# Row maximum of attention scores: a copy, three maxima and a 32x32 transpose replaced by one VectorE reduction with built-in transpose

## Chip, core and metric

The kernel runs on one core of one Trainium2 chip. The metric is the device time of one execution in microseconds, measured on that core. Engines are named as in the profile: PE is TensorE's matmul side and PEld its weight loads, DVE is VectorE, ACT is ScalarE, POOL is GpSimd, and SP is the queue that issues nearly all DMA transfers.

## The reference

Causal attention for 8 batches of 12 heads, 448 positions and a head width of 64, followed by a soft mixture of experts over all 3584 tokens:

```python
scores = scale * np.matmul(q, k.transpose(0, 1, 3, 2))
scores = np.where(mask, -1000000000.0, scores)          # causal
scores = scores - np.max(scores, axis=-1, keepdims=True)
attn = np.exp(scores)
attn = attn / (np.sum(attn, axis=-1, keepdims=True) + 1e-09)
attn_out = np.matmul(attn, v)
...
x = attn_out.transpose(0, 2, 1, 3).reshape(B * S, H * D)   # 3584 x 768
logits = x @ phi                                           # 32 slots, 4 per expert
d = exp(logits - logits.max(0)); d /= d.sum(0)             # dispatch
c = exp(logits - logits.max(1)); c /= c.sum(1)             # combine
slot_input = d.T @ x
for e in range(8):
    h = np.maximum(slot_input[e] @ w1[e], 0.0)
    slot_out[e] = h @ w2[e]
out = c @ slot_out
```

The change touches `np.max(scores, axis=-1)` only: for each query the maximum over its keys.

## The kernel before

**Two parts.** The first part runs over the 96 heads, two to a pair; the second runs the experts with their 64 weight tiles and writes the output. The logits and the dispatch of a batch are worked into the first part, by a table `plan` that says behind which head each piece stands.

**One head.** Scores are kept with keys on the partitions and queries in the columns. A head's tile `s` is one PSUM tile of 128 x 1024: the four chunks of 128 keys lie side by side, each only as wide as causality lets it be (448, 320, 192 and 64 queries), at the columns `SCOL`, so that 1024 columns are all used. There are three such tiles. `scores1` writes the mask (`c0`, `c12`, `c3`) and the products of the rounded `qd` and `ks` (`k0` to `k3`). Then the maximum of each query, over all keys, is taken in these steps:

- `max_evac` (`ev`): ACT copies chunk 0, 448 columns, out of PSUM to the SBUF tile `mx`.
- `max_keys` 0 to 2 (`x0` to `x2`): DVE takes the maximum of `mx` with chunks 1, 2 and 3 (320, 192 and 64 columns), in place. Each partition then holds the maximum of up to four keys.
- `max_keys` 3 (`x3`): DVE transposes `mx` in blocks of 32x32 to the tile `mt`; `max_keys` 4 (`x4`) reduces each block of 32 columns to one number. The result `r`, 128 x 14, holds for 14 blocks of 32 queries the maximum over each group of 32 partitions.
- `max_row` 0 (`mr0`): PE transposes `r` to `rt`; `max_row` 1 (`mr1`): DVE takes the maximum over the four groups, negated, to `mr`, 14 x 32.
- `max_spread` (`sp`): POOL spreads `mr` into 14 rows of the operand `r2`.

`scores2` (`t0` to `t3`) then adds to the same PSUM tile, by one more matmul per chunk with `k2` and `r2`, the negated maximum and the remainders of the rounding; `exps` on ACT takes the exponential to `pt`; `attv` (`a0` to `a3`) multiplies by v into the PSUM tile `po`; `norm` (`n0` to `n2`) on DVE divides by the sums. Beside this ACT rounds q and k of a later pair (`cq`, `ck`), POOL subtracts to get the remainders (`sq`, `sk`), and ACT copies `k2` (`c2`).

**The order.** Every engine runs its instructions as they stand in the program (the helper on L69 records each of them, which is why every row of the profile says L69). The table `ORDER` gives the order of the steps, one line for even heads and one for odd ones. The loop is pipelined: at head i it writes the scores of head i + 2 and takes their maxima, does `mr0`, `mr1` and `sp` of head i + 1, `scores2` and the exponential of head i, and `attv` and the normalisation of head i - 1. The heads 0 to 3 are written out by hand ahead of the loop and in its first two rounds.

**Loads.** SP issues its transfers in program order; one that has to wait for a buffer holds all behind it. The loads of q, k and v run up to three pairs ahead, through three buffers of the pool `raw` (3584 bytes per partition each). The weights come as tiles of 128 x 1536 (768 KB): tiles w0 to w22 have memory of their own and are loaded beside the attention. The next twelve, from w23 on, are put into the memory of the attention's own pools (`raw`, `fix`, `wk`, `xtp`, `moe`), which lie at one end of the SBUF one behind the other; each of these loads waits for the last users of whatever lies under its tile. `fix` holds the tiles that live through the whole attention, `mx` and `mt` among them (L106, L107).

Of the kernel before, what the change touches and what calls it, by code (L numbers as in the profile page):

```python
# [9 lines left out]
F32 = mybir.dt.float32  # L10
F32R = mybir.dt.float32r
BF16 = mybir.dt.bfloat16
AF = mybir.ActivationFunctionType
ALU = mybir.AluOpType
AX = mybir.AxisListType
PSUM = bass.MemoryType.PSUM

P = 128
NB, NH, S, HD = 8, 12, 448, 64
# [6 lines left out]
NQB = S // 32  # L26
# [4 lines left out]
NHD = 2 * NPAIR  # L31
# [13 lines left out]


ORDER = (
# [4 lines left out]
)  # L52

SC0, SC1, SC2, SC3 = 512, 0, 320, 960
CQ0 = (0, 128, 256, 384)
SCOL = (SC0, SC1, SC2, SC3)
# [28 lines left out]
def attention_soft_moe(ctx: ExitStack, tc: tile.TileContext, qk, va, phi, w1, w2, out):  # L85
    nc = _Core(tc)
# [6 lines left out]
    xtp = early.enter_context(tc.tile_pool(name="xtp", bufs=1, side="right"))  # L93
    wk = early.enter_context(tc.tile_pool(name="wk", bufs=1, side="right"))
    fix = early.enter_context(tc.tile_pool(name="fix", bufs=1, side="right"))
# [7 lines left out]
    qd_, ks_ = ([fix.tile([P, 2, S], F32R, name=f"{o}0")] for o in ("qd", "ks"))  # L103
    x_[1] = fix.tile([P, NCH, 3 * P], F32, name="x1")
    qd_.append(fix.tile([P, 2, S], F32R, name="qd1"))
    mx_ = fix.tile([P, S], F32, name="mx")  # L106
    mt_ = fix.tile([P, S], F32, name="mt")  # L107
    ks_.append(fix.tile([P, 2, S], F32R, name="ks1"))
    r2_ = [fix.tile([P, 2, S], F32R, name="r20")]
    va_[0] = fix.tile([P, NCH, 2, VC], F32, name="va0")  # L110
# [13 lines left out]
    st = {}  # L124
# [11 lines left out]
    def loads_v(p, eng=nc.sync):  # L136
        if p < NPAIR:
            eng.dma_start(out=va_[p % 2], in_=va[p])
# [49 lines left out]
    ident = const.tile([P, P], F32, name="ident")  # L188
# [8 lines left out]
    po0 = ps_1.tile([P, NCH, VC], F32, name="po")  # L197
    identb = const.tile([P, P], BF16, name="identb")

    zero = mt_[:, 0:P // 2]  # L200
    nc.vector.memset(zero, 0.0)
    nc.vector.tensor_copy(out=identb, in_=ident)
    for i in range(NR):
# [7 lines left out]
    def misc(name):  # L211
        return ps_1.tile([P, 512], F32, tag="m", name=name)
# [10 lines left out]
    def cast_q(p, hs=slice(0, 2)):  # L223
        if p < NPAIR:
            nc.scalar.activation(out=qd_[p % NR][:, hs], in_=st["raw", 0, p][:, hs], func=AF.Copy)

    def cast_k(p, hs=slice(0, 2)):
        if p < NPAIR:
            nc.scalar.activation(out=ks_[p % NR][:, hs], in_=st["raw", 1, p][:, hs], func=AF.Copy)
# [6 lines left out]
    def copy_k2(p, hs=slice(0, 2)):  # L236
        if p < NPAIR:
            nc.scalar.activation(out=k2_[64:P, hs], in_=ks_[p % NR][0:64, hs],
                                 func=AF.Copy)
# [35 lines left out]
        for part in ("c0", "k3", "c3", "c12", "k2", "k1", "k0"):  # L275
            scores1(i, part)

    def max_evac(i):
        if i < NHD:
            st["mx", i] = (xtp.tile([P, 512], F32, tag="xt", name="mx1", bufs=2)[:, 0:S] if i == 1  # L280
                           else mx_)
            nc.scalar.activation(out=st["mx", i], in_=st["s", i][:, SC0:SC0 + S], func=AF.Copy)

    def max_keys(i, k):
        if i >= NHD:
            return
        if k < 3:
            s, mx = st["s", i], st["mx", i]
            c, w = k + 1, S - CQ0[k + 1]
            nc.vector.tensor_tensor(out=mx[:, CQ0[c]:S], in0=s[:, SCOL[c]:SCOL[c] + w],  # L290
                                    in1=mx[:, CQ0[c]:S], op=ALU.max)
        elif k == 3:
            nc.vector.transpose(out=mt_, in_=st.pop(("mx", i)))
        else:
            r = st["r", i] = wk.tile([P, NQB], F32, tag="r", name=f"r{i}", bufs=2)
            nc.vector.tensor_reduce(out=r, in_=mt_.rearrange("p (b k)->p b k", k=32),
                                    axis=AX.X, op=ALU.max)

    def max_row(i, k):
        if i >= NHD:  # L300
            return
        if k == 0:
            st["rt", i] = misc(f"rt{i}")
            nc.tensor.transpose(out=st["rt", i][0:NQB, 0:P], in_=st.pop(("r", i)), identity=ident)
        else:
            mr = st["mr", i] = wk.tile([NQB, 32], F32, tag="mr", name=f"mr{i}", bufs=2)
            nc.vector.tensor_reduce(out=mr, in_=st.pop(("rt", i))[0:NQB, 0:P].rearrange("p (g t)->p t g", g=4),
                                    axis=AX.X, op=ALU.max, negate=True)

    def max_spread(i):  # L310
        if i >= NHD:
            return
        p, h = divmod(i, 2)
        mr = st.pop(("mr", i))

        nc.gpsimd.affine_select(out=r2_[p % NR][0:NQB, h].rearrange("p (b t)->p b t", t=32),
                                in_=mr.unsqueeze(1).to_broadcast([NQB, NQB, 32]),
                                compare_op=ALU.is_equal, fill=0.0, base=0,
                                pattern=[[-1, NQB], [0, 32]], channel_multiplier=1)
# [12 lines left out]
    def exps(i):  # L332
        if i < NHD:
            nc.scalar.activation(out=pt_[i % 2][:, 0:1024], in_=st.pop(("s", i)), func=AF.Exp, scale=SCALE)
# [108 lines left out]
    plan = {}  # L443
# [22 lines left out]
    scores1_all(0)  # L466
    warm(START[1])

    max_evac(0)
    cast_q(0, h1)  # L470
    sub_q(0, h1)
    scores1_all(1)
    warm(START[2])
    copy_k2(0, h0)
    max_evac(1)
    cast_k(1, h0)
    cast_k(1, h1)
    cast_q(1, h0)
    copy_k2(0, h1)
    cast_q(1, h1)  # L480

    for i, k in ((0, 0), (0, 1), (0, 2), (0, 3), (0, 4), (1, 0)):
        max_keys(i, k)
    sub_k(1, h0)
    max_row(0, 0)
    warm(START[5], po0.rearrange("p a b->p (a b)")[:, 0:2 * P])
    scores1_all(2)
    warm(START[3])
    max_evac(2)
    max_row(0, 1)  # L490
    max_spread(0)
    for k in (1, 2, 3, 4):
        max_keys(1, k)
    sub_q(1, h0)

# [27 lines left out]
    for i in range(NHD):  # L523
        p, h = divmod(i, 2)
        if h:
            load_qk(p + 3, 1)
            if p + 1 < NPAIR - 1:
                loads_v(p + 1)
            load_qk(p + 3, 0)
            if p % 2 and nload < RES:  # L530
                load_w(nload)
                nload += 1
        if i == NHD - 3:

            loads_v(NPAIR - 1, nc.scalar)
        if i < 2:
            scores2(i, (1, 0, 2))
            if i:
                scores1_all(3)
                max_evac(3)  # L540
            scores2(i, (3,))
            exps(i)
            if i == 0:
                max_row(1, 0)
                warm(START[4], po0.rearrange("p a b->p (a b)")[:, 0:P])
                max_row(1, 1)
                sub_k(1, h1, nc.vector)
                max_spread(1)
                sub_q(1, h1)

        qs = [int(n[1]) for n in ORDER[h] if n[0] == "a"]
        first = qs[:2] if qs[0] == 3 else qs[:1]
        for n in ORDER[h]:
            if i < 2 and (n in ("ev", "exp") or n[0] in "kt" or n in ("c0", "c3", "c12")):
                continue
            if i == 0 and n in ("mr0", "mr1", "sp"):
                continue
            if n[0] == "k" or n in ("c0", "c3", "c12"):
                scores1(i + 2, n)
            elif n[0] == "t":  # L560
                scores2(i, (int(n[1]),))
            elif n[0] == "a":
                attv(i - 1, (int(n[1]),), first)
            elif n[0] == "x":
                max_keys(i + 2, int(n[1]))
            elif n[0] == "n":
                norm(i - 1, int(n[1]))
            elif n in ("mr0", "mr1"):
                max_row(i + 1, int(n[2]))
            elif n == "ld":  # L570
                if i % 12 == 3 and i > 12:
                    logits_d(i // 12 - 1, lt)
            elif n == "plan":
                if later and i:
                    later.pop(0)()
                plan.get(i, int)()
            else:
                {"ev": lambda: max_evac(i + 2), "exp": lambda: exps(i), "sp": lambda: max_spread(i + 1),
                 "ck": lambda: cast_k(p + 2), "sk": lambda: sub_k(p + 2), "cq": lambda: cast_q(p + 2),
                 "c2": lambda: copy_k2(p + 1), "sq": lambda: sub_q(p + 2)}[n]()  # L580
        if i == NHD - 1:

            scs.close()
            pe = att.enter_context(tc.tile_pool(name="pe", bufs=1, space=PSUM, reuse_waits="tile"))
            ps = [pe.tile([P, 512], F32, name=f"e{k}") for k in range(6)]

    i, b, p = NHD - 1, NB - 1, NPAIR - 1
# [9 lines left out]
    for k, qcs in ((2, (3, 2)), (4, (1, 0))):  # L597
# [6 lines left out]
                                in1=sm[:, cs].unsqueeze(2).to_broadcast([P, 2, HD]), op=ALU.mult)  # L604
# [17 lines left out]
    for c in range(NCH):  # L622
# [11 lines left out]
                            axis=AX.X, op=ALU.min)  # L634
# [21 lines left out]
    for hf in range(2):  # L656
# [7 lines left out]
        else:  # L664
# [8 lines left out]
                            axis=AX.X, op=ALU.add)  # L673
# [139 lines left out]
    n = NBUF  # L813
# [83 lines left out]
```

## Time and profile before

| | |
|---|---|
| timed runs (3) | median 454.3 us, 453.79 to 455.17 |
| span of the profiled execution | 452.4 us; it states no other time |
| instructions | 12067 |
| PE, DVE and ACT busy, 0 to 15 us | 11.52, 9.49 and 10.48 us |
| the same, 15 to 42 us | 26.01, 23.88 and 23.58 us |
| the same, 344 to 380 us | 35.23, 21.83 and 10.69 us |
| the same, 380 to 452 us | 51.32, 28.59 and 21.22 us |
| DMA | 119.04 MB, 263 GB/s over the span |

The attention with its heads ends at about 344 us, the rest is the experts and the output. A row of a group gives the names of output and input with shapes, the number of instructions, then their busy time and the mean time of one, then the engine's idle time ahead of them and what ended most of it. A row of the timeline gives start and length, with idle time and releaser in brackets. In the rows of DMA issues the last number is the time from issue to landing. All times are microseconds, apart from the means, which are in nanoseconds.

### The profile page before, as it was taken

What the parts mean: (1) busy time and instruction counts of PE and PEld (TensorE: products, weight loads), DVE (VectorE), ACT (ScalarE), POOL (GpSimd) and SP (SyncE); (2) the same over time, 40 slices, a digit from 0 to 9 for tenths busy, and PEclk for the clock granted to TensorE, in tenths of its full rate; (3) what the DMA queues carried; (4) which work ended last, traced back from release to release, by engine and by line L of the source; (5) the groups of instructions that cost most, each with busy time, mean ns of one, the idle gap of its engine ahead of it and who ended that gap; (6) DMA issues with size and microseconds to landing.
All of it is one profiled execution on the core that took longest, in us unless ns stands there. A gap on an engine that the chain in (4) does not pass through costs nothing.

```text
span 452.4 us, 12067 instructions
## 1 busy us (share of the span) xinstructions
PE 426.1 (94%) x4628; PEld 365.6 (81%) x4628; DVE 348.6 (77%) x1050; ACT 329.8 (73%) x496; POOL 267.0 (59%) x216
## 2 busy tenths in 40 slices
PE   7999999999999999999999999999999999999750
PEld 3898999999999989998999899989998864544330
DVE  5888888888888888889888888888888457623450
ACT  6898899789988979897889789978995311333340
POOL 5988778777777777777777777877783000000000
PEclk9999999999999999999999999999999999999985
DMA  8377766776767766776577766776667999999998
GB/s 275 132 257 240 226 194 225 240 229 185 224 213 251 236 204 192 236 239 223 172 237 252 225 201 202 222 242 234 198 202 262 419 412 424 421 427 410 403 394 347
DMA packets 34473, 119.04 MB, mean 263 GB/s; under 512 B 3824, under 2 KB 8944, under 8 KB 32880
## 3 DMA queue, kind: packets, MB, share of 16 engines
q1 hardware_dynamic: 34272, 118.01, 74.7%
q8 instruction: 37, 0.61, 0.5%
q10 hardware_dynamic: 144, 0.27, 0.2%
q14 instruction: 20, 0.16, 0.1%
HBM read 107.25 MB, written 11.01 MB: 261 GB/s over the span
## 4 chain that ended last, share of the span: by engine, by line
PE 74%; DMA 12%; POOL 4%; DVE 3%; ACT 2%; issue 1%; SPq 0%; POOLq 0%; ACTq 0%
PE po L69 34%; PE s L69 24%; DMA w<-in_w_dram 10%; PE xt L69 4%; PE g L69 3%; PE sp L69 2%; POOL r L69 2%; PE rt L69 2%; DMA qk<-in_qk_dram 2%; PE e L69 1%; PE pp L69 1%; POOL ks L69 1%; DVE lm L69 1%; PE hp L69 1%; ACT ot L69 1%
## 5 line engine op out<-in xcount | busy, mean ns | idle before, releaser
L69 PE MATMUL po<-va,pt 128*128 128x65 f32 x1900 | 193.5, 250 | 0.1
L69 PEld LDWEIGHTS po<-va,pt 128*128 128x128 f32 x1900 | 190.5, 171 | 0.5 <-issue 0.3
L69 DVE TENSOR_TENSOR mx<-s,mx 128x320 f32<-128x320 f32 (+2 forms) x288 | 100.8, 350 | 30.2 <-ACT mx L69 26.4
L69 POOL TENSOR_TENSOR r<-qk,qd 64x896 fp32r<-64x896 f32 (+1 forms) x50 | 101.5, 2030 | 6.9 <-ACT qd L69 3.0
L69 POOL TENSOR_SCALAR_AFFINE_SELECT r<-mr 14x448 fp32r<-14x448 f32 x96 | 61.9, 645 | 72.1 <-DVE mr L69 71.6
L69 ACT ACTIVATE pt<-s 128x1024 f32<-128x1024 f32 x96 | 98.3, 1024 | 5.5 <-PE s L69 2.6
L69 POOL TENSOR_TENSOR ks<-qk,ks 64x896 fp32r<-64x896 f32 (+1 forms) x47 | 98.1, 2087 | 4.4 <-ACT ks L69 0.8
L69 PE MATMUL s<-r,k 128*128 128x320 f32 (+3 forms) x384 | 83.0, 298 | 1.4 <-POOL r L69 1.3
L69 ACT ACTIVATE mx<-s 128x448 f32<-128x448 f32 x96 | 52.5, 547 | 36.3 <-PE s L69 23.6
L69 PE MATMUL s<-qd,ks 128*128 128x448 f32 (+3 forms) x384 | 75.9, 308 | 1.5 <-ACT qd L69 1.4
L69 DVE STREAM_TRANSPOSE mt<-mx 128x448 f32<-128x448 f32 x96 | 62.0, 645 | 3.3
L69 PEld LDWEIGHTS s<-r,k 128*128 128x128 f32 (+1 forms) x384 | 60.0, 176 | 5.3 <-POOL r L69 2.0
L69 DVE TENSOR_REDUCE r<-mt 128x14 f32<-128x448 f32 x96 | 58.4, 609 | 0.1
L69 PEld LDWEIGHTS s<-qd,ks 128*128 128x128 f32 (+1 forms) x384 | 54.9, 180 | 3.0 <-ACT qd L69 2.2
L69 ACT ACTIVATE ks<-qk 128x896 fp32r<-128x896 f32 (+1 forms) x50 | 45.6, 914 | 2.8 <-DMA qk<-in_qk_dram 2.8
L69 ACT ACTIVATE k<-ks 64x896 fp32r<-64x896 f32 (+1 forms) x49 | 45.8, 935 | 1.1
L69 ACT ACTIVATE qd<-qk 128x896 fp32r<-128x896 f32 (+1 forms) x50 | 46.1, 922 | 0.5 <-DMA qk<-in_qk_dram 0.4
L69 PEld LDWEIGHTS <-identb 128*128 128x128 bf16 x339 | 29.1, 99 | 17.6 <-issue 15.1
L69 DVE TENSOR_TENSOR x<-po,sm 128x256 f32<-128x256 f32 x95 | 40.3, 424 | 3.3
L69 PE MATMUL s<-tri,identb 128*128 128x64 bf16 (+2 forms) x288 | 39.5, 234 | 0.2
L69 ACT ACTIVATE xts<-xt 128x512 f32<-128x512 f32 x47 | 28.2, 600 | 2.8 <-PE xt L69 0.5
L69 PE MATMUL xt<-ident,x 128*128 128x128 f32 x188 | 28.4, 274 | 0.0
(137 smaller groups left out, 398.7 us busy)
## 6 DMA issues: line engine op xcount, KB each, us to landing
qk<-in_qk_dram SPq DMA_DIRECT2D x94, 448.0 KB, 3.5
w<-in_w_dram SPq DMA_DIRECT2D x43, 768.0 KB, 6.1
w<-in_w_dram SPq DMA_DIRECT2D x10, 1536.0 KB, 19.3
va<-in_va_dram SPq DMA_DIRECT2D x47, 260.0 KB, 3.5
out_dram<-ot SPq DMA_DIRECT2D x16, 384.0 KB, 6.7
out_dram<-ot SPq DMA_DIRECT2D x2, 1536.0 KB, 9.2
qk<-in_qk_dram SPq DMA_DIRECT2D x4, 224.0 KB, 3.5
hw<-in_w_dram SPq DMA_DIRECT2D x1, 768.0 KB, 6.6
```

What stands on the lines that cost most here:

```text
L69: return self._tc.keep_in_program_order(op(*args, **kwargs))
```

## The change

ACT's copy is gone. DVE reduces straight from PSUM: `max_keys` 0 is one `tensor_reduce` over all 1024 columns, taken as 32 blocks of 32 and transposed 32x32 on the way (`apply_transpose=True`). Its result `r` is 128 x 32, one column for each block of 32 queries of each chunk. `max_keys` 1 to 3 then take the maximum of chunk 0's 14 columns (16 to 29) with those of the other chunks, over 10, 6 and 2 columns, in place. PE's transpose reads these 14 columns. `mx` and `mt` go; the tile of zeros that lay in `mt` gets one of its own.

```diff
-    ("c3", "c0", "k3", "c12", "k1", "k0", "k2", "t0", "t2", "ev", "x1", "t1", "a0", "a3", "t3", "ck",
-     "mr0", "exp", "x0", "a2", "mr1", "x2", "x3", "a1", "cq", "sp", "n0", "sk", "n1", "ld", "n2", "x4", "plan"),
+    ("c3", "c0", "k3", "c12", "k1", "k0", "k2", "t0", "t2", "t1", "a0", "a3", "t3", "ck",
+     "mr0", "exp", "x0", "a2", "x1", "x2", "x3", "mr1", "a1", "cq", "sp", "n0", "sk", "n1", "ld", "n2", "plan"),
...
-    mx_ = fix.tile([P, S], F32, name="mx")
-    mt_ = fix.tile([P, S], F32, name="mt")
+    zero = fix.tile([P, P // 2], F32, name="zero")
...
-    def max_evac(i):
-        if i < NHD:
-            st["mx", i] = (xtp.tile([P, 512], F32, tag="xt", name="mx1", bufs=2)[:, 0:S] if i == 1
-                           else mx_)
-            nc.scalar.activation(out=st["mx", i], in_=st["s", i][:, SC0:SC0 + S], func=AF.Copy)
...
-        if k < 3:
-            s, mx = st["s", i], st["mx", i]
-            c, w = k + 1, S - CQ0[k + 1]
-            nc.vector.tensor_tensor(out=mx[:, CQ0[c]:S], in0=s[:, SCOL[c]:SCOL[c] + w],
-                                    in1=mx[:, CQ0[c]:S], op=ALU.max)
-        elif k == 3:
-            nc.vector.transpose(out=mt_, in_=st.pop(("mx", i)))
+        if k == 0:
+            r = st["r", i] = wk.tile([P, 32], F32, tag="r", name=f"r{i}", bufs=2)
+            nc.vector.tensor_reduce(out=r, in_=st["s", i].rearrange("p (b k)->p b k", k=32),
+                                    axis=AX.X, op=ALU.max, apply_transpose=True)
         else:
-            r = st["r", i] = wk.tile([P, NQB], F32, tag="r", name=f"r{i}", bufs=2)
-            nc.vector.tensor_reduce(out=r, in_=mt_.rearrange("p (b k)->p b k", k=32),
-                                    axis=AX.X, op=ALU.max)
+            r, c0, c, q = st["r", i], SC0 // 32, SCOL[k] // 32, CQ0[k] // 32
+            rq = r[:, c0 + q:c0 + NQB]
+            nc.vector.tensor_tensor(out=rq, in0=rq, in1=r[:, c:c + NQB - q], op=ALU.max)
...
-            nc.tensor.transpose(out=st["rt", i][0:NQB, 0:P], in_=st.pop(("r", i)), identity=ident)
+            nc.tensor.transpose(out=st["rt", i][0:NQB, 0:P], in_=st.pop(("r", i))[:, SC0 // 32:SC0 // 32 + NQB], identity=ident)
...
-    max_evac(0)
...
-    for i, k in ((0, 0), (0, 1), (0, 2), (0, 3), (0, 4), (1, 0)):
+    for i, k in ((0, 0), (0, 1), (0, 2), (0, 3), (1, 0)):
         max_keys(i, k)
```

The odd line of `ORDER` changes in the same way, and the calls of `max_evac` for heads 1 to 3 in the start go as well. PE's order of instructions stays as it was; ACT and DVE have 96 fewer each.

On DVE, in the round of head 40, these rows stood between two normalisations before the change (`s42` is the tile of head 42, `mr41` belongs to head 41, `po`, `sm` and `x0` to the normalisation; what an instruction waits for is in brackets):

```order
L69 TENSOR_TENSOR x0_101<-po_129,sm38_2294 128x4x64 [waits DVE_49]
L69 TENSOR_REDUCE r41_2304<-mt_90 128x14
L69 TENSOR_TENSOR mx_89<-s42_2313,mx_89 128x192 [waits Activation_49]
L69 TENSOR_TENSOR mx_89<-s42_2313,mx_89 128x320 [waits DVE_49]
L69 TENSOR_REDUCE mr41_2340<-rt41_2333 14x32 [waits PE_49,Pool_49]
L69 TENSOR_TENSOR mx_89<-s42_2313,mx_89 128x64 [waits DVE_49]
L69 STREAM_TRANSPOSE mt_90<-mx_89 128x448 [waits DVE_49]
```

The same place after the change:

```order
L69 TENSOR_TENSOR x0_100<-po_128,sm38_2210 128x4x64 [waits DVE_49]
L69 TENSOR_REDUCE r42_2248<-s42_2227 128x32 [waits PE_49]
L69 TENSOR_TENSOR r42_2248<-r42_2248 128x10 [waits DVE_49]
L69 TENSOR_TENSOR r42_2248<-r42_2248 128x6 [waits DVE_49]
L69 TENSOR_TENSOR r42_2248<-r42_2248 128x2 [waits DVE_49]
L69 TENSOR_REDUCE mr41_2256<-rt41_2245 14x32 [waits PE_49,Pool_49]
L69 TENSOR_SCALAR sm39_2262<-po_128 128x4 [waits PE_49]
```

The reduction waits for PE instead of ACT, and all of the maximum of head 42 now stands ahead of `mr41`; before, the smallest maximum, the transpose and the reduction stood behind it.

On SP, at the end of the attention, the loads of the first weight tiles that overlie the attention's pools stood so before the change (`w22` is the last with memory of its own):

```order
L69 DMA w22_4981<-in_w2_dram 128x1536
L69 DMA w23_5332<-in_w2_dram 128x1536 [waits DMAHW5_49,DMAHW7_49,DMAHW3_49,Pool_49]
L69 DMA w24_5334<-in_w1_dram 128x1536 [waits DMAHW4_49,PE_49]
L69 DMA w25_5336<-in_w1_dram 128x1536 [waits DVE_49,PE_49,Activation_49]
L69 DMA w26_5338<-in_w1_dram 128x1536 [waits DMAHW6_49,PE_49]
L69 DMA w27_5340<-in_w1_dram 128x1536 [waits DVE_49,Activation_49]
```

The same loads after the change:

```order
L69 DMA w22_4793<-in_w2_dram 128x1536
L69 DMA w23_5138<-in_w2_dram 128x1536 [waits DMAHW3_49,Pool_49]
L69 DMA w24_5140<-in_w1_dram 128x1536 [waits DMAHW5_49,DMAHW7_49,DMAHW4_49,Pool_49]
L69 DMA w25_5142<-in_w1_dram 128x1536 [waits PE_49,Activation_49]
L69 DMA w26_5144<-in_w1_dram 128x1536 [waits DMAHW6_49,DVE_49,PE_49]
L69 DMA w27_5146<-in_w1_dram 128x1536 [waits PE_49]
```

No line of the diff names these loads. They move because `fix` has become 3328 bytes smaller per partition (two tiles of 1792 go, one of 256 comes) and the two tiles `r` together with their pool 128 larger, so that the `raw` buffers behind them lie 3200 bytes elsewhere. Before, w23 overlay one `raw` buffer and most of the next, among them those of q and k of the last pair, 47; now it overlies part of the one that held q of pair 46, and w24 takes the last pair's. The waits for POOL are the subtractions of q: that of pair 47 for w23 before and for w24 now, that of pair 46 for w23 now.

The raw buffers also rotate otherwise at the start, as the loads of q and k of the pairs 2 and 3 and of `phi` show. Before:

```order
L69 DMA qk1_2_115<-in_qk_dram 128x896
L69 DMA qk0_2_117<-in_qk_dram 128x896 [waits DMAHW2_49,DMAHW0_49,DVE_49]
L69 DMA phi0_232<-in_phi_dram 128x96 [waits DMAHW1_49]
L69 DMA phi1_233<-in_phi_dram 128x96
L69 DMA qk1_3_280<-in_qk_dram 128x896 [waits DMAHW3_49,Pool_49]
```

After:

```order
L69 DMA qk1_2_114<-in_qk_dram 128x896
L69 DMA qk0_2_116<-in_qk_dram 128x896 [waits DMAHW1_49,DMAHW3_49,DMAHW0_49,Pool_49]
L69 DMA phi0_225<-in_phi_dram 128x96
L69 DMA phi1_226<-in_phi_dram 128x96 [waits DMAHW2_49]
L69 DMA qk1_3_272<-in_qk_dram 128x896 [waits DVE_49]
```

The load of q of pair 2 waits for POOL's subtraction of q of pair 0, second head, where it waited for DVE's subtraction of k.

More of the change, by code (lines that the diff above doesn't have):

```diff
@@ L198, in attention_soft_moe @@
     identb = const.tile([P, P], BF16, name="identb")
-    zero = mt_[:, 0:P // 2]
     nc.vector.memset(zero, 0.0)
@@ L474, in attention_soft_moe @@
     copy_k2(0, h0)
-    max_evac(1)
     cast_k(1, h0)
@@ L488, in attention_soft_moe @@
     warm(START[3])
-    max_evac(2)
     max_row(0, 1)
     max_spread(0)
-    for k in (1, 2, 3, 4):
+    for k in (1, 2, 3):
         max_keys(1, k)
@@ L539, in attention_soft_moe @@
                 scores1_all(3)
-                max_evac(3)
             scores2(i, (3,))
@@ L553, in attention_soft_moe @@
         for n in ORDER[h]:
-            if i < 2 and (n in ("ev", "exp") or n[0] in "kt" or n in ("c0", "c3", "c12")):
+            if i < 2 and (n == "exp" or n[0] in "kt" or n in ("c0", "c3", "c12")):
                 continue
@@ L577, in attention_soft_moe @@
             else:
-                {"ev": lambda: max_evac(i + 2), "exp": lambda: exps(i), "sp": lambda: max_spread(i + 1),
+                {"exp": lambda: exps(i), "sp": lambda: max_spread(i + 1),
                  "ck": lambda: cast_k(p + 2), "sk": lambda: sub_k(p + 2), "cq": lambda: cast_q(p + 2),
```

4 rows, old and new, of the table ORDER are left out of this document.

## The prediction

> **What bounds the kernel now.** I read the page's busy shares and its chain of work first, then the busy time by stages, then the rows of single instructions around the edges of the stages.
>
> ```profile
> PE 426.1 (94%) x4628; PEld 365.6 (81%) x4628; DVE 348.6 (77%) x1050; ACT 329.8 (73%) x496; POOL 267.0 (59%) x216
> ...
> PE 74%; DMA 12%; POOL 4%; DVE 3%; ACT 2%; issue 1%; SPq 0%; POOLq 0%; ACTq 0%
> ```
>
> TensorE (PE) holds three quarters of the chain, the DMA most of the rest. VectorE (DVE), where the change works, is busy for 77% but holds 3%. A mean over the span hides the stages, so here are some stretches. The columns are length, then busy time (and instructions) of PE, PEld, DVE, ACT and POOL, then the granted clock, the DMA share and GB/s.
>
> ```profile
> 42.00:340.00 298.00, 298.00 (x3272) 278.65 (x3264) 261.17 (x792) 261.70 (x374) 227.93 (x168) 1.00 0.69 220
> ...
> 341.40:344.10 2.70, 2.70 (x32) 2.47 (x28) 2.40 (x6) 1.00 (x2) 1.79 (x1) 1.00 0.00 0
> 344.10:348.00 3.90, 3.90 (x52) 3.60 (x51) 3.39 (x12) 2.21 (x4) 0.68 (x2) 1.00 0.96 331
> ...
> 352.00:366.00 14.00, 13.75 (x184) 10.78 (x186) 6.13 (x25) 4.05 (x10) 0.00 (x0) 1.00 1.02 414
> ```
>
> From 42 to 340 us PE is busy for 298.00 of 298 us at full clock: it is the bound, and time taken from DVE or ACT there is worth nothing. Ahead of that lies a start in which PE waits for its first inputs. Behind it, from about 344 us, the DMA queue is full: the expert weights stream at over 400 GB/s, and whatever brings that stream forward brings the end forward. The change must therefore be priced at three places: in the steady heads, at the start, and where the stream begins. The row of 341.40 to 344.10 already shows the odd thing: the DMA idles for 2.7 us right ahead of the stretch in which it is short.
>
> **The steady heads.** These DVE and ACT groups go (busy time, mean ns of one):
>
> ```profile
> L69 DVE TENSOR_TENSOR mx<-s,mx 128x320 f32<-128x320 f32 x96 | 47.1, 490 | 16.4 <-ACT mx L69 14.4
> L69 DVE TENSOR_TENSOR mx<-s,mx 128x192 f32<-128x192 f32 x96 | 34.3, 357 | 13.7 <-ACT mx L69 11.9
> L69 DVE TENSOR_TENSOR mx<-s,mx 128x64 f32<-128x64 f32 x96 | 19.5, 203 | 0.1
> L69 DVE STREAM_TRANSPOSE mt<-mx 128x448 f32<-128x448 f32 x96 | 62.0, 645 | 3.3
> L69 DVE TENSOR_REDUCE r<-mt 128x14 f32<-128x448 f32 x96 | 58.4, 609 | 0.1
> ...
> L69 ACT ACTIVATE mx<-s 128x448 f32<-128x448 f32 x96 | 52.5, 547 | 36.3 <-PE s L69 23.6
> ```
>
> DVE loses 490 + 357 + 203 + 645 + 609 = 2304 ns per head, ACT 547 ns. What comes has no row of its own; the nearest are these:
>
> ```profile
> L69 DVE STREAM_TRANSPOSE hw<-hsb 128x256 f32<-128x256 f32 x6 | 2.7, 446 | 0.2
> L69 DVE TENSOR_REDUCE bm<-lt 128x1 f32<-128x128 f32 x7 | 2.0, 286 | 0.2
> L69 DVE TENSOR_TENSOR run_m<-run_m,bm 128x1 f32<-128x1 f32 x7 | 2.1, 307 | 0.2
> L69 DVE TENSOR_TENSOR rz<-run_z,wc 128x1 f32<-128x1 f32 x1 | 0.2, 151 | 0.0
> ```
>
> Transposes grow by (645 - 446)/192 = 1.04 ns a column, so one of 1024 columns would take 645 + 576 x 1.04 = 1.24 us. Reduces grow by (609 - 286)/320 = 1.01 ns, which gives 609 + 576 x 1.01 = 1.19 us. If transpose and reduction share one pass, the new instruction takes 1.19 to 1.24 us; if they are two passes, the sum, 2.43. I take **1.24**, the row of the transpose, because nothing else that this unit does with a column costs much over 1 ns. The maxima over 10, 6 and 2 elements lie between 151 and 307 ns; I take 0.19 us for each, near the lower row and with its wait for the one before. Per head DVE goes from 2.30 to 1.24 + 3 x 0.19 = 1.81 us, some 0.5 us less, and over 96 heads ACT loses 52.5 us. All of it lies beside PE at 298.00 of 298, so it counts **0**.
>
> That holds only while the maxima stay off the path. In the new order all three stand ahead of the reduce mr of the next head, which PE's scores wait for by way of POOL. One head, from the timeline (start, us):
>
> ```profile
> 200.62 0.69 PE L69 MATMUL s<-qd,ks 128*128 128x448 f32 x3
> ...
> 203.13 0.27 DVE L69 TENSOR_REDUCE mr<-rt 14x32 f32<-14x128 f32 x1
> 203.47 0.64 POOL L69 TENSOR_SCALAR_AFFINE_SELECT r<-mr 14x448 fp32r<-14x448 f32 x1 [0.81 <-DVE mr L69]
> ...
> 204.63 0.39 PE L69 MATMUL s<-r,k 128*128 128x448 f32 x1
> ```
>
> The tile is done at 200.62 + 0.69 = 201.31, and mr starts 1.82 us later. After the change it starts some 1.24 + 0.57 = 1.81 us later: a tie. POOL's spread ends at 203.47 + 0.64 = 204.11 and PE uses it at 204.63, so 0.52 us are spare. The new reduce can take up to 1.24 + 0.52 + 0.02, some 1.78 us, before this head waits; the 1.24 lies well below. I take this head for all 96. What is queued behind mr on DVE, the normalisation of the head before, comes no later either. The exponential now waits for DVE too, but for a reduce of two heads earlier, long done: 0.
>
> **The start.** ACT loses the first copies, some 1 us, so the casts may come earlier.
>
> ```profile
> 9.57 1.14 POOL L69 TENSOR_TENSOR ks<-qk,ks 64x448 fp32r<-64x448 f32 x1 [0.82 <-ACT ks L69]
> ...
> 10.24 0.28 DVE L69 TENSOR_REDUCE mr<-rt 14x32 f32<-14x128 f32 x1
> ...
> 10.78 0.64 POOL L69 TENSOR_SCALAR_AFFINE_SELECT r<-mr 14x448 fp32r<-14x448 f32 x1
> ...
> 14.39 0.94 ACT L69 ACTIVATE qd<-qk 128x896 fp32r<-128x896 f32 x1
> ...
> qk<-in_qk_dram SPq DMA_DIRECT2D x1, 448.0 KB, 4.8
> ```
>
> POOL's subtraction at 9.57 waited 0.82 us for ACT and could go up to 0.8 us earlier. But the spread behind it needs the first mr, and on DVE that now stands behind the whole reduce of tile 1 instead of one maximum of 490 ns. Stepping tile 0 and tile 1 through with the durations above, mr starts at 10.3 instead of 10.24; the later ones of the start move by the same few hundredths. So POOL, in program order, gains nothing: **+0.1 us**, between -0.2 and +0.5. On SP, the load of q of pair 2 now waits for POOL's subtraction of pair 0's second head, with the phi loads, one more qk load and va behind it in the same queue. It leaves about 1.2 us later; that tile's cast ran at 14.39 with no idle time ahead of it, on data that the load issued at 7.31 had landed 4.8 us later (last row), at 12.1: 2.3 us of cover, so 0 (at most +1.1 if all the delay fell on the cast).
>
> **Where the stream begins.** The pool of fixed tiles shrinks by 3328 bytes per partition while the r tiles grow by 128, so the three raw q/k buffers lie 3200 bytes elsewhere against the weight tiles that overlie them. As the rows of SP show, w23 loses its waits for the raw buffer of the last pair and w24 takes them. In the trace of before:
>
> ```profile
> 337.37 0.43 SPq L69 DMA_DIRECT2D w<-in_w_dram  x1
> ...
> 343.21 0.33 SPq L69 DMA_DIRECT2D w<-in_w_dram  x1
> ...
> 362.38 0.33 SPq L69 DMA_DIRECT2D w<-in_w_dram  x1
> ...
> 341.07 2.11 POOL L69 TENSOR_TENSOR r<-qk,qd 64x896 fp32r<-64x896 f32 x1
> ...
> w<-in_w_dram SPq DMA_DIRECT2D x1, 768.0 KB, 4.3
> ...
> w<-in_w_dram SPq DMA_DIRECT2D x1, 768.0 KB, 6.4
> ```
>
> The issue at 337.37 is w22, that at 343.21 is w23: it leaves when POOL's last subtraction of q, at 341.07 + 2.11 = 343.18, is over. After the change w23 waits for the subtraction one pair earlier, done before 337, and can go at once, at about 337.8. The 2.7 us in which the DMA idled take it: 768 KB, at the 414 GB/s of the row above (786 KB in decimal units), are 1.9 us. From 343.2 on w24 and all behind it follow one tile further on. Does the advance survive to the end? An alone transfer lands 4.3 us after its issue (first of the two landing rows); the issue at 362.38 needed 6.4, so 2.1 us of queue stood in front of it. That is the least of all issues up to the end, and over 1.9, so the queue never runs dry: **-1.9 us**.
>
> **Sum.** 452.4 - 1.9 + 0.1 = 450.6 us of span. The profile states only its span; the three timed runs have a median of 454.3 and lie 1.4 to 2.8 above it. I carry the difference over: 454.3 - 1.8 = **452.5 us**, with a range of its own of 451.8 to 453.2. About 0.3% (1.4 us) is what a measurement of this kernel can tell from no change, so below 452.9 counts as faster.
>
> **Rivals.** (1) The change does what it says, but the advance gets lost: w23 still waits, or the later tiles wait for buffers that PE frees, not for the queue. For it speaks that PE is busy for 13.75 of 14 us even in the stretch with a full DMA; against it that the landing times lie over 4.3 us throughout. Then 454.3, up to 455 with the loss of the start. (2) The slower side: the reduce runs its 1024 columns in two passes or at half rate, 2.3 to 2.43 us. The remaining DVE rows of a head are these:
>
> ```profile
> L69 DVE TENSOR_REDUCE mr<-rt 14x32 f32<-14x128 f32 x96 | 25.9, 269 | 2.1 <-PE rt L69 2.0
> ...
> L69 DVE TENSOR_SCALAR sm<-po 128x4 f32<-128x4 f32 x95 | 11.7, 124 | 2.9 <-PE po L69 2.9
> ...
> L69 DVE RECIPROCAL sm<-sm 128x4 f32<-128x4 f32 x95 | 16.9, 178 | 3.3
> ...
> L69 DVE TENSOR_TENSOR x<-po,sm 128x256 f32<-128x256 f32 x95 | 40.3, 424 | 3.3
> ```
>
> A head would need 2.43 + 0.57 + 0.27 + 0.12 + 0.18 + 0.42 = 3.99, some 4.1 with the gaps, against 343.18 / 96 = 3.57 that a head takes now, since POOL's last work for the heads ends at 343.18: 0.53 x 96, about 51 us. That gives 454.3 + 51 - 1.9, about 503 us. It decides from 1.78 us of reduce on. [...] (3) Faster than forecast: the relieved ACT shortens the start, by up to the 0.8 us that POOL waited and what follows from it; then about 451.3.
>
> **Chances.** Forecast 0.58 (0.50 of it below 452.9, 0.08 within 0.3%); rival 1 0.20 (0.18 within, 0.02 slower); rival 2 0.12; rival 3 0.10. So faster 0.60, within 0.26, slower 0.14. A range of 451.0 to 454.9 takes in the forecast, rival 1 and most of rival 3; rival 2 is left out.
>
> **What would show it.** The row r<-s at about 1.24 us, the maxima r<-r below 0.2; PE still busy for all of 42 to 340; SP's second weight issue of that region at 337.8 instead of 343.21, and the idle stretch of the DMA filled; landings and end some 1.9 us earlier. A reduce over 1.78 us, PE waiting for POOL ahead of s<-r,k, or a w23 issued at 343 would make the prediction wrong.

## The result, and the profile after

The changed kernel takes 468.26 us (median of 4 runs, 467.12 to 471.85) against 454.34: 1.0314 times as long, with a 95% interval of 1.0286 to 1.0342. The forecast was 452.5. Its profiled execution spans 466.0 us, 13.6 more than that of before.

First the page after: busy shares and the chain of work that ended last, by engine.

```profile
PE 429.8 (92%) x4628; PEld 368.3 (79%) x4628; DVE 338.5 (73%) x954; ACT 288.5 (62%) x400; POOL 266.7 (57%) x216
...
PE 69%; DVE 14%; DMA 12%; issue 1%; ACT 1%; SPq 0%
```

DVE is busy for 10 us less than before, and yet its share of the chain has grown from 3% to 14%: it has less to do and is waited for more. The stretch in which PE had no gap, after the change (columns as before):

```profile
42.00:340.00 298.00, 289.84 (x3159) 271.07 (x3160) 241.70 (x686) 218.13 (x279) 220.01 (x163) 1.00 0.65 214
```

The waits of PE in that stretch, after (us in total, times, longest):

```profile
PE xt L69 <- DVE mr L69: 7.0, 7, 1.0
PE s L69 <- POOL r L69: 0.8, 1, 0.8
```

PE is idle for 298.00 - 289.84 = 8.16 us there. 7.0 of them are seven waits of 1.0 us for mr, one for each of the first seven batches. It is not the scores that wait: the spread by way of POOL costs 0.8 us in all, so the slack that the forecast gave the scores held. It is the transposes xt, which need the one PSUM tile from which mr still has to read rt.

The groups of DVE instructions in question, after:

```profile
L69 DVE TRANSPOSE_TENSOR_REDUCE r<-s 128x32 f32<-128x1024 f32 x96 | 119.9, 1249 | 26.5 <-PE s L69 23.9
...
L69 DVE TENSOR_TENSOR r<-r 128x10 f32<-128x10 f32 x96 | 24.1, 252 | 3.3
L69 DVE TENSOR_TENSOR r<-r 128x6 f32<-128x6 f32 x96 | 18.8, 196 | 3.3
...
L69 DVE TENSOR_TENSOR r<-r 128x2 f32<-128x2 f32 x96 | 15.8, 164 | 3.3
...
L69 DVE TENSOR_TENSOR run_m<-run_m,bm 128x1 f32<-128x1 f32 x7 | 9.0, 1288 | 0.2
```

The big reduction takes 1249 ns, as forecast, and the three maxima 612 ns together where 570 were forecast. (These are means: the maximum over 128x10 takes between 0.15 us and, in the timeline at 43.05, 1.58 us.) The surprise is the last row, an instruction that the change does not touch: the running maximum of the logits over 128x1, which took 307 ns before, now takes 1288, seven times. One of the seven places, in the timeline after (DVE, then POOL, then PE):

```profile
68.20 1.30 DVE L69 TENSOR_TENSOR run_m<-run_m,bm 128x1 f32<-128x1 f32 x1
69.42 1.24 DVE L69 TRANSPOSE_TENSOR_REDUCE r<-s 128x32 f32<-128x1024 f32 x1
...
71.18 0.28 DVE L69 TENSOR_REDUCE mr<-rt 14x32 f32<-14x128 f32 x1
...
67.38 2.11 POOL L69 TENSOR_TENSOR ks<-qk,ks 64x896 fp32r<-64x896 f32 x1
...
71.51 0.66 PE L69 MATMUL xt<-ident,x 128*128 128x128 f32 x4 [1.02 <-DVE mr L69]
```

run_m ends at 68.20 + 1.30 = 69.50, and POOL's subtraction at 67.38 + 2.11 = 69.49. In all seven batches the two ends lie 0.01 to 0.02 us apart. The same instruction and the same subtraction in the kernel before:

```profile
65.15 0.30 DVE L69 TENSOR_TENSOR run_m<-run_m,bm 128x1 f32<-128x1 f32 x1
...
63.34 2.10 POOL L69 TENSOR_TENSOR ks<-qk,ks 64x896 fp32r<-64x896 f32 x1
```

There, too, the ends lie together, at 65.45 and 65.44. run_m was held before the change already, but it came to the end of the subtraction and lost 0.15 us (e7 below shows that it takes 0.16 us by itself). Now it comes 0.8 us after the subtraction's start and waits for the rest of it.

The start shows the same on the new maxima. After (the "x3" is the three maxima in one row), with POOL beside it:

```profile
15.23 2.68 DVE L69 TENSOR_TENSOR r<-r 128x10 f32<-128x10 f32 x3
...
14.50 1.15 POOL L69 TENSOR_TENSOR r<-qk,qd 64x448 fp32r<-64x448 f32 x1
15.61 2.08 POOL L69 TENSOR_TENSOR ks<-qk,ks 64x896 fp32r<-64x896 f32 x1
```

Three instructions that need some 0.5 us (the same three take 0.56 at 19.10, where POOL runs nothing) take 2.68, first behind one subtraction and then behind the next. In the kernel before, two of the old maxima ran wholly beside that same subtraction of k and were not held:

```profile
16.41 0.88 DVE L69 TENSOR_TENSOR mx<-s,mx 128x320 f32<-128x320 f32 x2
...
15.47 2.10 POOL L69 TENSOR_TENSOR ks<-qk,ks 64x896 fp32r<-64x896 f32 x1
```

They take 0.88 us, which is their usual 490 and 357 ns with the gap between them. What tells the two kinds apart is where the operands lie. The old maxima read the scores from PSUM and mx from SBUF; the new ones read r twice from SBUF, as run_m reads run_m and bm.

How much of the time lies where is read from POOL's own rows. One subtraction of k in the timeline before:

```profile
42.19 2.10 POOL L69 TENSOR_TENSOR ks<-qk,ks 64x896 fp32r<-64x896 f32 x1
```

The same one after, and the last subtraction of q, which started at 341.07 before:

```profile
46.02 2.09 POOL L69 TENSOR_TENSOR ks<-qk,ks 64x896 fp32r<-64x896 f32 x1
...
354.93 2.09 POOL L69 TENSOR_TENSOR r<-qk,qd 64x896 fp32r<-64x896 f32 x1
```

So 46.02 - 42.19 = 3.8 us are lost up to there, 354.93 - 341.07 - 3.83 = 10.0 in the rest of the attention, and 13.6 - 13.9 = -0.3 behind it: the start and the steady heads are the loss, and of the gain forecast for the end little shows. (Of the 10.0 us, 8.16 are idle time of PE. Its busy time has grown too, from 426.1 to 429.8 us in all, with the same instructions; their ends are modelled, so part of a wait can appear as busy time.)

### The profile page after: what moved, and what is told of

Its sections match the earlier page's. It is cut to its first block, busy times and chain, and to the rows that moved or that the text cites. A ratio compares the mean times of both kernels' runs of the same rounds, so it can differ in the third digit from the quotient of the medians.

```text
span 466.0 us, 11818 instructions
## 1 busy us (share of the span) xinstructions
PE 429.8 (92%) x4628; PEld 368.3 (79%) x4628; DVE 338.5 (73%) x954; ACT 288.5 (62%) x400; POOL 266.7 (57%) x216
## 4 chain that ended last, share of the span: by engine, by line
PE 69%; DVE 14%; DMA 12%; issue 1%; ACT 1%; SPq 0%
PE po L69 31%; PE s L69 21%; DMA w<-in_w_dram 11%; DVE r L69 7%; PE xt L69 5%; PE sp L69 2%; DVE run_m L69 2%; PE g L69 2%; PE rt L69 2%; PE pp L69 1%; PE e L69 1%; DVE x L69 1%; DVE sm L69 1%; PE hp L69 1%; DMA qk<-in_qk_dram 1%
## 5 line engine op out<-in xcount | busy, mean ns | idle before, releaser
L69 DVE TRANSPOSE_TENSOR_REDUCE r<-s 128x32 f32<-128x1024 f32 x96 | 119.9, 1249 | 26.5 <-PE s L69 23.9
L69 DVE TENSOR_TENSOR r<-r 128x10 f32<-128x10 f32 (+2 forms) x288 | 58.7, 204 | 9.8
L69 PE MATMUL xt<-ident,x 128*128 128x128 f32 x188 | 29.9, 282 | 7.7 <-DVE mr L69 7.4
L69 DVE TENSOR_SCALAR sm<-po 128x4 f32<-128x4 f32 x95 | 15.1, 159 | 23.1 <-PE po L69 22.7
L69 DVE TENSOR_REDUCE mr<-rt 14x32 f32<-14x128 f32 x96 | 26.7, 278 | 2.5 <-PE rt L69 2.2
```

Of the source, the lines that this page charges most:

```text
L69: return self._tc.keep_in_program_order(op(*args, **kwargs))
```

## The experiments

The theory, "held by POOL": a DVE instruction with two inputs in SBUF that starts while POOL runs a subtraction (which reads SBUF) is held until the subtraction ends, and what stands behind it on DVE is late by as much. The first rival, "order": the time is lost because mr now stands behind the whole maximum of the next tile. All times of before are from the same chips, 454.16 to 454.19.

**e1, the running maximum as a reduction.** bm is written beside run_m, and one reduction takes the minimum of the two columns:

```diff
-        nc.vector.tensor_tensor(out=mn, in0=mo, in1=st.pop(("bm", b)), op=ALU.min)
+        nc.vector.tensor_reduce(out=mn, in_=run2[(b + 1) % 2], axis=AX.X, op=ALU.min)
```

> The changed kernel, but the running maximum of the logits (run_m, 128x1, once per batch) is taken by a reduction over two neighbouring columns instead of a two-input tensor_tensor. Theory 'held by POOL': run_m takes 1.29 us instead of 0.31 because both of its inputs lie in SBUF and it waits for the end of POOL's subtraction; with one input it takes about 0.2 us, the seven stalls of PE at xt (1.0 us each) go, and 7 x 1.27 = 8.9 us come back: about 459.4 us. Rival 'order': the time is lost because mr now stands behind the whole maximum of the next tile on DVE; then run_m is a symptom and the time stays at 467 to 468.

460.1 us (1.0136 of before, 1.0119 to 1.0153), where 459.4 was expected. The group in e1:

```profile
L69 DVE TENSOR_REDUCE run_m<-run_m 128x1 f32<-128x2 f32 x7 | 1.1, 155 | 0.2
```

The stretch from 42 to 340 us in e1:

```profile
42.00:340.00 298.00, 297.48 (x3246) 278.73 (x3245) 240.11 (x704) 225.01 (x289) 226.16 (x167) 1.00 0.66 220
```

155 ns instead of 1288, and PE's idle time falls from 8.16 to 0.52 us, though mr stands where it stood. "Order" alone is out. (The heads are not quite back: as the table below shows, they still lose 2.1 us, part of which PE's modelled ends may show as busy time.)

**e2, the maxima as reductions.** One transposing reduction per chunk into a row of 14, padded with -3e38, then one reduction over the four rows:

```diff
-            nc.vector.tensor_reduce(out=r, in_=st["s", i].rearrange("p (b k)->p b k", k=32),
-                                    axis=AX.X, op=ALU.max, apply_transpose=True)
-        else:
-            r, c0, c, q = st["r", i], SC0 // 32, SCOL[k] // 32, CQ0[k] // 32
-            rq = r[:, c0 + q:c0 + NQB]
-            nc.vector.tensor_tensor(out=rq, in0=rq, in1=r[:, c:c + NQB - q], op=ALU.max)
+            for c in (3, 1, 0, 2):
+                s, q = st["s", i][:, SCOL[c]:SCOL[c] + S - CQ0[c]], CQ0[c] // 32
+                nc.vector.tensor_reduce(out=rc_[i % 2][:, c, q:NQB], in_=s.rearrange("p (b k)->p b k", k=32),
+                                        axis=AX.X, op=ALU.max, apply_transpose=True)
+        elif k == 1:
+            r = st["r", i] = wk.tile([P, NQB], F32, tag="r", name=f"r{i}", bufs=2)
+            nc.vector.tensor_reduce(out=r, in_=rc_[i % 2].rearrange("p c b->p b c"), axis=AX.X, op=ALU.max)
```

> The changed kernel, but its three small two-input maxima go: one transposing reduction per chunk into a row padded with -3e38, then one reduction over the four rows. No maximum of the scores has two SBUF inputs any more; run_m stays as it is. DVE per head gets some 0.2 us longer. Theory 'held by POOL': the maxima that took 0.4 to 1.6 us in the first twelve heads and at one head per batch lose that, some 3.5 us: about 464.5. Rival 'order': mr stands behind even more work, so 468 or more.

458.84 us (1.0104, 1.0089 to 1.0119): the direction is the theory's, the size is not; 464.5 was expected. run_m is still held, but for less, and PE's seven waits for mr are shorter. The group in e2:

```profile
L69 DVE TENSOR_TENSOR run_m<-run_m,bm 128x1 f32<-128x1 f32 x7 | 7.9, 1132 | 0.2
```

PE's waits from 42 to 340 us in e2:

```profile
PE xt L69 <- DVE mr L69: 5.0, 7, 0.7
```

The expectation counted 3.5 us for the held maxima, and 9.4 came back. In e2's timeline the subtraction of k that started at 42.19 before starts at 41.52: the start does not only lose its 3.8 us but runs 0.7 ahead of the kernel before, with run_m untouched. So it is the held maxima that cost the start. The last subtraction of q starts at 345.11, so the heads lose 4.7 us instead of 10.0; run_m is held for 0.16 us less, and PE's waits for mr fall from 7.0 to 5.0 us.

**e3, both edits.**

> Both edits: no DVE instruction of the steady heads has two SBUF inputs. Theory 'held by POOL': PE is busy without a break again from 42 to 340 us, and the time is that of the kernel before within 1.5 us: 453 to 456. Rival 'order': 468 or more.

453.43 us (0.9985, 0.9971 to 0.9998), and 453.36 when it ran again as e10 (0.9985, 0.9969 to 1.0001). The stretch of PE in e3:

```profile
42.00:340.00 298.00, 298.00 (x3267) 278.87 (x3266) 233.25 (x794) 226.98 (x291) 228.94 (x169) 1.00 0.67 222
```

298.00 of 298 again. The last subtraction of q in e3's timeline:

```profile
339.64 2.10 POOL L69 TENSOR_TENSOR r<-qk,qd 64x896 fp32r<-64x896 f32 x1
```

It starts 1.4 us earlier than in the kernel before (341.07). With no DVE instruction of two SBUF inputs left in these heads, the whole loss is gone, with one more DVE instruction per head than in the changed kernel. e10 was this kernel once more:

> Kernel e3 once more, as the partner of e9 on the same chip: 453.0 to 453.9 by either theory.

**e4, mr ahead of the three maxima.**

```diff
-     "mr0", "exp", "x0", "a2", "x1", "x2", "x3", "mr1", "a1", "cq", "sp", "n0", "sk", "n1", "ld", "n2", "plan"),
+     "mr0", "exp", "x0", "a2", "mr1", "x1", "x2", "x3", "a1", "cq", "sp", "n0", "sk", "n1", "ld", "n2", "plan"),
...
-     "x1", "x2", "x3", "mr1", "sp", "a2", "a1", "n0", "ld", "n1", "n2", "sq", "c2", "plan"),
+     "mr1", "x1", "x2", "x3", "sp", "a2", "a1", "n0", "ld", "n1", "n2", "sq", "c2", "plan"),
```

> The changed kernel with mr of the next head moved to stand right behind the big reduction and ahead of the three small maxima. Rival 'order': mr then starts 1.25 us behind the tile, earlier than in the kernel before (1.82), and the time falls to about 454.5. Theory 'held by POOL': the small maxima no longer delay mr, but run_m still does, by 1.0 less the 0.6 us that mr gains: 461 to 464.

456.37 us (1.0051, 1.0036 to 1.0066): a miss for "held by POOL", which had 461 to 464, and nearly what "order" had. The two groups in e4:

```profile
L69 DVE TENSOR_TENSOR r<-r 128x6 f32<-128x6 f32 x96 | 57.6, 600 | 3.3
...
L69 DVE TENSOR_TENSOR run_m<-run_m,bm 128x1 f32<-128x1 f32 x7 | 4.9, 707 | 0.2
```

The stretch from 42 to 340 us in e4:

```profile
42.00:340.00 298.00, 298.00 (x3271) 279.90 (x3271) 267.27 (x709) 226.71 (x292) 228.37 (x169) 1.00 0.68 221
```

The holds have not gone: the second maximum is now long in nearly every head (600 ns in the mean against 196; POOL's spread starts as soon as mr is done, and in 90 of the 96 heads the two end within 0.01 us of each other), run_m is still held for more than half a microsecond. But nothing that PE needs soon stands behind them, and PE has no gap. Both are needed for the loss: an instruction that is held, and behind it one that PE waits for. My expectation took the remaining hold of run_m to reach PE in full; the 0.6 us that mr gained, and some spare time before PE wants it, seem to have taken all of it.

The profiled execution of e4 was the longest of its four (457.39 us), and the granted clock (the last column but two) was low for a while in its start, so its start can't be compared with that of the others:

```profile
20.00:25.00 5.00, 5.00 (x37) 4.90 (x36) 3.91 (x13) 1.87 (x2) 3.92 (x5) 0.66 0.27 81
```

**e11, the two smallest edits**, e1 and e4 together:

> The changed kernel with the two smallest edits: the running maximum as a reduction (e1) and mr ahead of the three small maxima (e4). The small maxima keep two SBUF inputs and are still held by POOL, but nothing that PE waits for stands behind them. Theory: only the loss of the start is left, as in e4: 455.5 to 456.4. If a held maximum still reaches PE in the steady heads, 458 or more.

456.31 us (1.0047, 1.0026 to 1.0067), within the expected range, and PE is busy for 298.00 of 298 us from 42 to 340 in e11 as well. But the range was met by luck. It counted on the loss of the start, and in e11's profiled execution (456.31 us, a span of 454.5) the attention ends where it ended before, its last subtraction of q starting at 341.22 against 341.07:

```profile
341.22 2.11 POOL L69 TENSOR_TENSOR r<-qk,qd 64x896 fp32r<-64x896 f32 x1
...
353.76 0.41 PE L69 MATMUL po<-va,pt 128*128 128x65 f32 x2 [1.00 <-DMA va<-in_va_dram]
```

So 454.5 - 452.4 - 0.15 = 1.9 of the 2.1 us lie behind the attention's last subtraction. One wait of PE there, the second row, is 1.00 us long. The view puts it down to a load of va, but the last of these was issued at 337.19 and had landed 2.7 us later, so what released PE, and why e3 does not have the 1.9 us, stays open.

**e7, POOL's part taken away.** run_m keeps its two SBUF inputs; POOL leaves out the subtraction of k in the seven rounds in question:

```diff
-                 "ck": lambda: cast_k(p + 2), "sk": lambda: sub_k(p + 2), "cq": lambda: cast_q(p + 2),
+                 "ck": lambda: cast_k(p + 2), "sk": lambda: None if i % 12 == 2 and i > 2 else sub_k(p + 2), "cq": lambda: cast_q(p + 2),
```

> The changed kernel without POOL's subtraction of k in the seven rounds in which run_m is taken (it leaves out the rounding remainders of k for seven of the 48 pairs). run_m keeps its two SBUF inputs. Theory 'held by POOL': run_m takes 0.31 us or less, and 7 x 1.27 = 8.9 us come back: about 459.4. If run_m is long by itself, or because of the reduction behind it, it stays at 1.29 us and the time at 467 to 468.

460.02 us (1.0121, 1.0091 to 1.015); 459.4 was expected. The group in e7:

```profile
L69 DVE TENSOR_TENSOR run_m<-run_m,bm 128x1 f32<-128x1 f32 x7 | 1.1, 160 | 0.2
```

e1 took away the second SBUF input, e7 took away POOL; either brings run_m to some 0.16 us and the time to 460. So it takes both sides.

**e8, the hold without the new instruction.** In the kernel before, the reduction of mt moves behind the running maximum, which so comes earlier into POOL's subtraction:

```diff
-     "mr0", "exp", "x0", "a2", "mr1", "x2", "x3", "a1", "cq", "sp", "n0", "sk", "n1", "ld", "n2", "x4", "plan"),
+     "mr0", "exp", "x0", "a2", "mr1", "x2", "x3", "a1", "cq", "sp", "n0", "sk", "n1", "ld", "n2", "plan", "x4"),
...
-     "x1", "mr1", "x2", "x3", "sp", "a2", "a1", "n0", "ld", "n1", "n2", "sq", "c2", "x4", "plan"),
+     "x1", "mr1", "x2", "x3", "sp", "a2", "a1", "n0", "ld", "n1", "n2", "sq", "c2", "plan", "x4"),
```

> The kernel before the change, with the reduction of mt moved behind the logits' running maximum, so that run_m starts 0.55 us earlier, in the middle of POOL's subtraction. Theory 'held by POOL': run_m grows from 0.31 to about 0.87 us and ends with the subtraction, in a kernel without the new instruction; PE's slack of 0.5 to 0.8 us takes most of it, time 454 to 456. If the new reduction causes the long run_m, it stays at 0.31.

456.63 us (1.0044, 1.0029 to 1.0059), 0.6 over the upper end. The group in e8:

```profile
L69 DVE TENSOR_TENSOR run_m<-run_m,bm 128x1 f32<-128x1 f32 x7 | 5.9, 839 | 0.2
```

One of the seven places in e8's timeline, DVE and POOL:

```profile
64.44 0.83 DVE L69 TENSOR_TENSOR run_m<-run_m,bm 128x1 f32<-128x1 f32 x1
...
63.15 2.10 POOL L69 TENSOR_TENSOR ks<-qk,ks 64x896 fp32r<-64x896 f32 x1
```

PE's waits from 42 to 340 us in e8:

```profile
PE rt L69 <- DVE r L69: 3.2, 7, 0.5
```

839 ns, as the theory had it, and again it ends with the subtraction (65.27 and 65.25): the new reduction is not needed for a hold. The cost was more than expected because here it is the reduction r, moved behind run_m, that PE waits for at rt.

**Where the time lies in each run.** The starts of two subtractions on POOL, in us, cut each profiled execution in two: that of k at 42.19 before, and the last one of q.

| run | k | last q | lost up to k | lost between |
|---|---|---|---|---|
| before | 42.19 | 341.07 | | |
| after | 46.02 | 354.93 | 3.8 | 10.0 |
| e1, run_m as a reduction | 45.14 | 346.16 | 3.0 | 2.1 |
| e7, no subtraction beside run_m | 46.44 | 347.25 | 4.3 | 1.9 |
| e2, maxima as reductions | 41.52 | 345.11 | -0.7 | 4.7 |
| e3, both | 41.24 | 339.64 | -1.0 | -0.5 |
| e4, mr ahead | 44.88 | 343.74 | 2.7 | 0.0 |
| e11, mr ahead and run_m as a reduction | 42.80 | 341.22 | 0.6 | -0.5 |

The savings in the heads do not add up: taking away either hold saves part of what the other costs. The start differs from run to run even where its instructions are the same (after, e1 and e7: 3.0 to 4.3), so a single profile gives its loss to about a microsecond.

**e5, e9 and e6: the loads at the end.** e5 adds a dummy tile to e3 so that the raw buffers lie where they lay before:

```diff
     zero = fix.tile([P, P // 2], F32, name="zero")
+    fix.tile([P, 728], F32, name="padn")
```

> Kernel e3 (both edits) with a dummy tile of 2912 bytes in the pool of fixed tiles, so that the raw q/k buffers lie where they lay before the change: w23 waits again for POOL's last subtraction and is issued some 6 us behind w22. If issuing w23 early is worth the 1.9 us of its transfer, e3 loses them here: about 455.3 us. If the advance is lost before the end, because the later tiles wait for buffers that PE frees, the time is that of e3: 453.0 to 453.9.

453.19 us (0.9973, 0.9958 to 0.9988). That settles nothing, because the raw buffers rotate otherwise and w23 still left early, at 337.86. e9 therefore issues w24, which waits for POOL's last subtraction, ahead of w23:

```diff
-    for n in range(RES, NBUF):
+    pre[RES] = slot(RES, f"w{RES}")
+    for n in (RES + 1, RES, *range(RES + 2, NBUF)):
         load_w(n)
```

> Kernel e3 with the loads of w23 and w24 issued in the other order. w24 waits for POOL's last subtraction, so the DMA idles again ahead of it as in the kernel before, and w23 comes one tile later. (e5 did not do this: its raw buffers rotate otherwise, and w23 still left early.) If the early w23 is worth its 1.9 us, this takes 1.9 more than e3 in the same call; if the advance is lost before the end, within 0.5 of it.

452.88 us (0.9962, 0.9948 to 0.9977) against 453.36 for e10 on the same chip: the kernel whose w23 comes late is no slower. Two stretches of e9 first, then the same of e10 (the last number is GB/s):

```profile
344.00:360.00 16.00, 15.50 (x174) 13.65 (x170) 7.64 (x29) 6.84 (x11) 1.48 (x3) 1.00 1.00 400
360.00:370.00 10.00, 10.00 (x165) 6.24 (x164) 5.30 (x22) 1.40 (x6) 0.00 (x0) 1.00 1.03 419
```

```profile
344.00:360.00 16.00, 15.54 (x172) 13.59 (x169) 7.52 (x31) 7.03 (x11) 1.48 (x3) 1.00 1.01 392
360.00:370.00 10.00, 10.00 (x161) 6.24 (x163) 5.43 (x23) 1.21 (x5) 0.00 (x0) 1.00 1.00 375
```

In e10 the stream moves 375 GB/s from 360 to 370 us, in e9 419, with PE busy for all of it in both. The early tile's lead of 0.79 MB shrinks by 10 us x 44 GB/s = 0.44 MB there, and by 16 us x 8 GB/s = 0.13 before. The loads behind the early tile do not move forward with it. One of them, issue and time to landing, in e9 and then in e10:

```profile
361.28 0.33 SPq L69 DMA_DIRECT2D w<-in_w_dram  x1
...
w<-in_w_dram SPq DMA_DIRECT2D x1, 768.0 KB, 6.3
```

```profile
361.01 0.33 SPq L69 DMA_DIRECT2D w<-in_w_dram  x1
...
w<-in_w_dram SPq DMA_DIRECT2D x1, 768.0 KB, 5.0
```

Both leave at the same place, 19.2 and 19.1 us after the end of POOL's last subtraction of q, because SP waits for a buffer that PE frees (the view of SP's waits names PE there, 2.3 us in both). The early tile makes the queue ahead of this load shorter, 5.0 us to landing instead of 6.3, where the lone transfer at 337.37 before took 4.3. Why the stream also moves fewer bytes while its queue is shorter is not settled: the DMA's busy share is 1.00 all the same.

e6 moves mr ahead in e3:

> Kernel e3 with mr moved ahead of the last reduction over the four rows. PE does not wait for mr in e3's steady heads any more, so nothing is to be had there; in the start up to 0.3 us. 453.0 to 453.9 by either theory; under 452.5 would show that mr is still late somewhere.

453.4 us (0.997, 0.9951 to 0.9989): nothing more is to be had from mr.

## Why the prediction was wrong

**The bound** was read rightly: PE in the heads (busy for 298.00 of 298 us before), the DMA stream behind (414 GB/s from 352 to 366 us). So were the price of the big reduction (1.24 us forecast for one pass, 1249 ns measured) and the slack of the scores: rival 2, the reduction in two passes with 2.3 to 2.43 us, did not come about. The trace names the instruction TRANSPOSE_TENSOR_REDUCE, and e2's pieces of 192 and 448 columns take 340 and 606 ns, (606 - 340)/256 = 1.04 ns a column, as the plain transpose does in the kernel before, with 645 and 446 ns for 448 and 256 columns.

**The step that failed** is the one that counted everything on DVE as **0** because it lay beside PE, after stepping one head through and taking "this head for all 96". DVE was stepped through by its own durations, but not against POOL, which held it (run_m for 1288 ns instead of 160). The size of the three maxima was near in the mean (612 ns against 570); what was missing is that the new maxima read SBUF twice where the old ones read PSUM and SBUF, and that the shorter path to run_m brought it 0.8 us into a subtraction instead of to its end. The head that was looked at, at 200.62, has no run_m ahead of its mr. In the heads from 42 us on, that is seven waits of 1.0 us at xt, which needs the PSUM tile that mr has to leave; my list of those who wait for mr had the scores only.

The sign stood in the trace of before. I took run_m's 307 ns from a row without asking what stretched it: it was itself a held instruction, 0.15 us above the 155 to 160 ns that it takes when nothing holds it (e1, e7), and it ended together with POOL's subtraction.

The runs show the hold from both sides: run_m takes 1288 ns beside POOL's subtraction and ends 0.01 to 0.02 us after it, 160 ns without that subtraction (e7), and 155 as a reduction (e1). What holds it inside the chip was not shown. None of the prediction's rivals had such a hold.

**The start**, forecast at +0.1 us between -0.2 and +0.5, cost 3.8, for the same reason: ahead of the steady heads the three maxima took up to 2.68 us. A gain such as rival 3 saw there seems to exist once nothing is held: e3's start is 1.0 us shorter than that of the kernel before, its attention ends 1.4 us earlier, and it spans 451.0 us against 452.4. That it comes from the relieved ACT was not tested.

**The stream's start**, forecast at -1.9 us, failed as well. w23 did leave at once (after the change SP issued w22 at 350.88 and w23 right behind it at 351.40), but the lead is given back before the end; e9 against e10 puts its worth at nothing, -0.5 us if anything. "So the queue never runs dry" rested on the 6.4 us of the issue at 362.38, called the least of all up to the end. That was misread: the issue at 350.01 in the same trace landed after 5.9. And the loads behind w23 are issued when PE has freed their buffers, early tile or not, as e9 and e10 show: this is the second half of rival 1, and it did come about.

**The sum** of the forecast, -1.8, so became +13.6 in the profiled execution: 3.8 in the start, 10.0 in the heads, and -0.3 behind them instead of -1.9.

## What to carry to other kernels

Ask of every DVE instruction where its inputs lie and what POOL does at that time: here two maxima that read PSUM and SBUF took their usual 490 and 357 ns beside a subtraction of POOL, while run_m, which reads SBUF twice, was held for the rest of one (1288 ns instead of 160). Before a duration is taken from a row, see whether its instructions end together with one of another engine. In e4 maxima held to 600 ns cost PE nothing from 42 to 340 us, as nothing urgent stood behind them in DVE's queue, so either turn a held instruction into a reduction (155 ns in e1) or put the urgent one ahead. And ask of a transfer that starts earlier whether those behind it can follow: here they waited for buffers, and w23's early start was worth nothing (453.36 us in e10, 452.88 in e9 without it).

## What the runs showed that was not expected

A DVE instruction over one column, 160 ns by itself (e7), took 1288 ns beside POOL's subtraction of 2.1 us. A change that took 10 us of work from DVE made DVE's share of the chain grow from 3% to 14%. And 96 maxima held to 600 ns in the mean (e4) cost PE nothing in the stretch from 42 to 340 us. The hold seems to go the other way too: in the start of the kernel before, POOL's spread begins 0.05 us after the start of a subtraction on DVE with two SBUF inputs, and takes 1.08 us instead of its usual 0.64. No run tests this by itself.

```profile
13.14 0.62 DVE L69 TENSOR_TENSOR ks<-qk,ks 64x448 fp32r<-64x448 f32 x1
...
13.19 1.08 POOL L69 TENSOR_SCALAR_AFFINE_SELECT r<-mr 14x448 fp32r<-14x448 f32 x1 [0.53 <-DVE mr L69]
```
